# Two small reorderings of a hand-written instruction order: global value products ahead of a routing step, and score steps of the second attention block behind FFN steps

## The chip, the cores and the metric

The kernel runs on one core of a Trainium2 chip. The metric is the device time of one execution in microseconds (us); the time before is the median of three runs. The core has five engines that each work through their own list of instructions in order and wait for one another by semaphores: TensorE (PE in the profile, with its weight loads as PEld), VectorE (DVE), ScalarE (ACT), GpSimd (POOL) and SyncE (SP), which starts most transfers.

## The reference

Three stages follow one another, all in float32:

- **Attention** over 4 batches, 8 heads, 512 local and 32 global tokens per head, head size 64. A local token sees the 32 global keys and the local keys at a distance of at most 32; a global token sees all 544 keys. Softmax, then the product with the values.
- **A dense FFN** on the 2176 resulting tokens of width 512: `h = x @ w_in` (2048 wide), `g = relu(h)**2`, `g @ w_out`.
- **Routed experts**: a token with `x @ w_skip > 0` goes to the one of 8 experts (512 to 1024 to 512, ReLU) with the highest logit `x @ w_gate`, and gets `x + p * y`, where `p` is the softmax probability; the others pass through.

## The kernel before

**Tiles.** Local tokens are cut in 16 tiles of 128, two to a block (`j` = 0 to 7, 256 tokens, `BLK`). Attention runs a tile at a time (`attention(t)`), the FFN a block at a time (`ffn_block(j)`), the routing a tile at a time (`route(t)`); the 32 global tokens of a batch are done in `attention_global(b)`, four heads at a time (`g` = 0, 1). The experts come after all of it, with tokens gathered by index.

**Products in two halves.** Operands of the FFN are split in a high half (`gh`, `xh`, written by a ScalarE cast) and the rest (`gl`, `xl`, a subtraction on GpSimd or VectorE: helper `split`, L203 and L204). A step of the FFN has a first part (`first(f)`: 12 matmuls into `h`, L803 to L805, then a ReLU on ScalarE, L807) and later a second part (`second(f)`: 6 matmuls of 512 columns with `gh` and `gl`, L828 to L830, into `acc`). Between them stand the square (L844 on VectorE or L846 on ScalarE) and the split.

**The order.** Every stage is a generator, and a string of letters says which one moves on by one step: `SEQ` for the start and blocks 0 and 1, `EVEN` for the blocks 2, 4 and 6, `ODD` for 3, 5 and 7. All engines take their order from it, since one step issues instructions on several engines and each engine runs its own in the order in which they were issued. In `SEQ`, `F1`, `E1`, `H1`, `I1` are the next step of the FFN of block 1 (F and I square on VectorE, E and H on ScalarE; F and E subtract on GpSimd, H and I on VectorE), `2a` and `2b` are steps of attention on tiles 4 and 5 (block 2), `R00` and `R01` are routing steps of tiles 0 and 1, `C`, `D` and `A` convert weights, `V` loads values. In `EVEN`, `F` and `E` are FFN steps of the block, `a`, `b`, `g` steps of the attention of the next block, `r` and `s` routing steps of the block before, `V` loads values.

**Steps that matter here.** A call of the FFN in `SEQ` issues by turns the first part of step n, and the square and split of step n with the second part of step n - 1 (in `EVEN` that of step n - 2). Step 1 of `attention` issues the score matmuls (L484), then for the first half: add mask (L497), maximum (L501, L502), four exponentials on ScalarE (L505); the softmax of the second half is step 2. Step 1 of `route` transposes (L300) and casts the high third (L713); step 2 makes the other thirds on VectorE (L703 to L705, and once L719 and on for the weights `w27`); step 3 multiplies (`pl`, L725), then a chain of small VectorE operations (L731 to L747); step 4 has the two prefix matmuls `pr` (L750, L751) and the chain L752 to L776; step 5 the matmul `pt` (L779). Step 3 of `attention_global` has the value products `gpo` and their eviction:

```python
po = ps.tile([P, D], F32, tag=O_TAG, bufs=BANKS[O_TAG], name=f"gpo{b}_{g}")
for c in range(TPB + 1):
    for hh in range(4):
        ...
        nc.tensor.matmul(po[cols, :], ...)
for hh in range(4):
    own = slice(SG * hh, SG * (hh + 1))
    nc.vector.tensor_scalar(
        out=xg[b * SG:(b + 1) * SG, 4 * g + hh], in0=po[own, :], scalar1=rs[own, 2:3], scalar2=None, op0=ALU.mult
    )
```

**Buffers.** `BANKS = {"tr": 2, "s": 1, "o": 1, "h": 2, "x2": 2}` gives the PSUM buffers by tag. In `EVEN`, `gpo`, `pl`, `pr` and `pt` all take the single buffer of tag `o`, in the order in which they are issued: a tile in it can be written only when the one before has been read. `h` of the FFN alternates between two buffers.

Of the kernel before, what the change touches and what calls it, by code (L numbers as in the profile page):

```python
# [22 lines left out]
    0b A V 0a W 0b V A 1q W W A 0b V 1a W W F0 A W E0 1a W W A W V 1a A F0 W 1a I0 A 1b L9 1a H0 V A A W V E0 W 1a  # L23
    X0 H0 A A E0 H0 W H0 A H0 W 1b E0 Lg1 A A W W A E0 1b W H0 A 1b E0 A H0 A E0 Lv00 A W W W 1g A I0 C 1b A 1g I0 W
    A D H0 Lv01 1g W E0 A E0 A I0 1g W C C 1g C W E0 A 1g Lq2 C Lk10 A H0 1g I0 2q A C C F0 2G Lk11 E0 I0 20 C 1b E0 21
    22 F0 F1 23 C D F0 H1 C C V R00 2a F1 D H1 E1 2a E1 D R00 2a H1 R00 R01 C H1 C C F1 I1 R01 V 2b R01 E1 D A F1
    2a E1 D C H1 2b F1 R00 2a I1 C C H1 D F1 V H1 R00 V F1 R01 C Lq3 E1 D E1 C C R01 F1 2b D C 2b H1 C C 1g F1 H1 2b
    2a E1 F1 D E1 F1 H1 Lv10 V 2b I1 V
"""

EVEN = """
    q E F F r E r a F a E lg F s F r E s E F g a s E a E a F g F r V a F g E r V E lv1 F b g s E F b E E b E V g b F
    b F b F g F s lk1 F g E V g lq F lk0 E
"""

# [1673 lines left out]
```

## Time and profile before

| what | value |
|---|---|
| time, median of 3 runs | 692.17 us (690.86 to 692.66) |
| time of the profiled execution | 692.0 us |
| span of the profiled execution, first to last instruction | 690.3 us |
| mean granted TensorE clock | 0.983 |
| busy share PE / PEld / DVE / ACT / POOL | 96 / 80 / 61 / 50 / 26% |

The page gives for each engine its busy time, then the span in 40 slices of 17.3 us (busy tenths, granted TensorE clock in tenths of full speed, transfers). The timeline of the trace lists single instructions of all engines in order of time with their start and duration, and in brackets how long the engine sat idle before one, and for whom it waited. The waits view sums those idle times.

### The profile page before, as it was taken

How to read it: one execution, taken by the hardware profiler on the slowest of the kernel's cores; microseconds unless marked ns; L12 is line 12 of the kernel's file. 1: busy time of each engine (PE TensorE's matmuls, PEld its weight loads, DVE VectorE, ACT ScalarE, POOL GpSimd, SP SyncE). 2: the span in 40 equal slices, each digit the busy share in tenths (PEclk: the TensorE clock that was granted, in tenths of full speed). 3: DMA queues.
4: the chain of work that ended last, by engine and by line, in shares of the span. 5: the costliest groups of instructions: out<-in, count | busy, mean ns of one | idle time of the engine just before them, and what ended most of it. 6: DMA issues, size and time to landing. Idle time of an engine off the chain costs nothing. (4 is left out here: it accounts for less than half of the span.)

```text
span 690.3 us, 16621 instructions
## 1 busy us (share of the span) xinstructions
PE 663.4 (96%) x6545; PEld 553.0 (80%) x6545; DVE 423.2 (61%) x1142; ACT 344.4 (50%) x834; POOL 180.7 (26%) x236
## 2 busy tenths in 40 slices
PE   6689999999999999999999999999999999999996
PEld 4466668788888888888888888888987887898875
DVE  1899983874566377367456647535248535816984
ACT  5767567765534444453445453434344324615862
POOL 8000043354222212312222322222212242301321
PEclk8699999999999999999999999999999999999999
DMA  9999844047053441307243402210056588953920
GB/s 274 248 294 249 282 99 109 1 109 149 5 120 65 95 109 36 85 2 149 72 76 90 108 6 85 82 63 32 1 153 192 200 286 300 385 204 111 371 94 21
DMA packets 137503, 93.39 MB, mean 135 GB/s; under 512 B 103541, under 2 KB 110709, under 8 KB 137412
## 3 DMA queue, kind: packets, MB, share of 16 engines
q1 hardware_dynamic: 127104, 70.62, 38.2%
q10 hardware_dynamic: 8292, 15.48, 6.8%
q0 software_dynamic: 2016, 6.09, 2.5%
q8 instruction: 55, 0.90, 0.6%
q14 instruction: 36, 0.29, 0.1%
HBM read 79.91 MB, written 12.66 MB: 134 GB/s over the span
## 5 line engine op out<-in xcount | busy, mean ns | idle before, releaser
L204 POOL TENSOR_TENSOR gl<-g,gh 128x256 fp32r<-128x256 f32 x107 | 79.8, 746 | 238.7 <-ACT gh L203 94.5
L803 PE MATMUL h<-xh,w_in 128*128 128x256 f32 x464 | 134.1, 289 | 0.0
L805 PE MATMUL h<-xh,w_in 128*128 128x256 f32 x464 | 129.8, 280 | 0.2 <-POOL w_in L275 0.2
L804 PE MATMUL h<-xl,w_in 128*128 128x256 f32 x464 | 129.6, 279 | 0.0
L828 PE MATMUL acc<-w_out,gh 128*128 128x512 f32 x232 | 97.0, 418 | 1.2 <-ACT gh L203 1.2
L830 PE MATMUL acc<-w_out,gl 128*128 128x512 f32 x232 | 91.9, 396 | 0.2
L829 PE MATMUL acc<-w_out,gh 128*128 128x512 f32 x232 | 91.5, 395 | 0.0
L803 PEld LDWEIGHTS h<-xh,w_in 128*128 128x128 f32 x464 | 87.1, 188 | 4.5 <-issue 1.0
L804 PEld LDWEIGHTS h<-xl,w_in 128*128 128x128 f32 x464 | 87.2, 188 | 2.7 <-DVE xl L204 0.2
L805 PEld LDWEIGHTS h<-xh,w_in 128*128 128x128 f32 x464 | 87.1, 188 | 0.4 <-POOL w_in L275 0.4
L807 ACT ACTIVATE g<-h 128x256 f32<-128x256 f32 x128 | 48.7, 380 | 66.8 <-PE h L805 45.1
L203 ACT CAST gh<-g 128x256 fp32r<-128x256 f32 x116 | 47.1, 406 | 37.7 <-DVE g L844 35.6
L844 DVE TENSOR_TENSOR g<-h,g 128x256 f32<-128x256 f32 x53 | 22.1, 417 | 69.5 <-ACT g L807 69.4
L505 ACT ACTIVATE sm<-sm,mx 128x128 f32<-128x128 f32 x120 | 41.2, 391 | 43.1 <-DVE mx L502 43.1
L830 PEld LDWEIGHTS acc<-w_out,gl 128*128 128x128 f32 x232 | 43.5, 188 | 12.0 <-POOL gl L204 1.5
L828 PEld LDWEIGHTS acc<-w_out,gh 128*128 128x128 f32 x232 | 43.6, 188 | 8.4 <-ACT gh L203 1.7
L829 PEld LDWEIGHTS acc<-w_out,gh 128*128 128x128 f32 x232 | 43.7, 189 | 5.8
L275 POOL TENSOR_TENSOR w_in<-st_raw_in,w_in 128x512 fp32r<-128x512 f32 x10 | 13.2, 1326 | 74.7 <-ACT w_in L271 74.7
L497 DVE TENSOR_TENSOR sm<-sc,masks_slots 128x512 f32<-128x512 f32 x30 | 20.6, 687 | 14.7 <-PE sc L484 13.5
L846 ACT ACTIVATE g<-g 128x256 f32<-128x256 f32 x63 | 26.2, 415 | 4.1 <-ACT g L807 2.1
L826 PE MATMUL acc<-st_raw_out,gh 128*128 128x512 f32 x48 | 23.9, 618 | 0.8 <-ACT gh L846 0.8
L511 PE MATMUL ptr<-ident,sm 128*128 128x128 f32 x120 | 20.5, 290 | 2.5 <-ACT sm L505 2.4
(649 smaller groups left out, 1446.3 us busy)
## 6 DMA issues: line engine op xcount, KB each, us to landing
st_e<-in_moe_w_dram SPq DMA_DIRECT2D x46, 512.0 KB
st_raw_in<-in_moe_w_in_dram SPq DMA_DIRECT2D x16, 512.0 KB
st_raw_out<-in_moe_w_out_dram SPq DMA_DIRECT2D x16, 512.0 KB
st_e<-in_moe_w_dram ACTq DMA_DIRECT2D x12, 512.0 KB
x2d<-x ACTq DMA_DIRECT2D x19, 256.5 KB
vr<-in_v_l_dram SPq DMA_DIRECT2D x32, 128.0 KB
st_gv<-in_v_l_dram SPq DMA_DIRECT2D x8, 512.0 KB
out_dram<-x ACTq DMA_DIRECT2D x16, 256.0 KB
```

What stands on the lines that cost most here:

```text
L203: nc.scalar.copy(hi, src)
L204: (lo_engine or nc.vector).tensor_tensor(out=lo, in0=src, in1=hi.bitcast(F32), op=ALU.subtract)
L505: nc.scalar.activation(sm[:, hh, :], sm[:, hh, :], AF.Exp, bias=mx[:, hh:hh + 1], scale=SCALE, **sums)
L803: nc.tensor.matmul(h, lhsT=wh, rhs=xh[:, k, :], start=(k == 0), stop=False)
L804: nc.tensor.matmul(h, lhsT=wh, rhs=xl[:, k, :], start=False, stop=False)
L805: nc.tensor.matmul(h, lhsT=wl, rhs=xh[:, k, :], start=False, stop=(k == KD - 1))
L807: nc.scalar.activation(g, h, AF.Relu)
L826: nc.tensor.matmul(acc[z], lhsT=gh[:, c], rhs=w, start=first_one, stop=last_one)
L828: nc.tensor.matmul(acc[z], lhsT=gh[:, c], rhs=wh, start=first_one, stop=False)
L829: nc.tensor.matmul(acc[z], lhsT=gh[:, c], rhs=wl, start=False, stop=False)
L830: nc.tensor.matmul(acc[z], lhsT=gl[:, c], rhs=wh, start=False, stop=last_one)
L846: nc.scalar.activation(square, g, AF.Square)
```

## The change

Only the order strings change; nothing is computed differently, and no transfer changes its place on SP's or any other queue.

```diff
-    22 F0 F1 23 C D F0 H1 C C V R00 2a F1 D H1 E1 2a E1 D R00 2a H1 R00 R01 C H1 C C F1 I1 R01 V 2b R01 E1 D A F1
-    2a E1 D C H1 2b F1 R00 2a I1 C C H1 D F1 V H1 R00 V F1 R01 C Lq3 E1 D E1 C C R01 F1 2b D C 2b H1 C C 1g F1 H1 2b
+    22 F0 F1 23 C D F0 H1 C C V R00 F1 2a D H1 E1 2a E1 D R00 2a H1 R00 R01 C H1 C C F1 I1 R01 V R01 E1 2b D A F1
+    2a E1 D C H1 F1 2b R00 2a I1 C C H1 D F1 V H1 R00 V F1 R01 C Lq3 E1 D E1 C C R01 F1 2b D C 2b H1 C C 1g F1 H1 2b
...
-    q E F F r E r a F a E lg F s F r E s E F g a s E a E a F g F r V a F g E r V E lv1 F b g s E F b E E b E V g b F
+    q E F F r E r a F a E lg F s F r E s E F g a s E a E a F g F g r V a F E r V E lv1 F b g s E F b E E b E V g b F
```

**In `EVEN` (three blocks) on TensorE.** `gpo` are the global value products, `pr` the prefix matmuls of the routing, `h_8` and `acc` the FFN. The piece of the difference for block 2, around the end of the first part of FFN step 8:

```order
 L805 MATMUL h_8_2784<-xh_2260,w_in_2_2131 128x256
+L626 MATMUL gpo_0_2799<-st_gv_0_2328,gpT_0_2778 32x64 x16
+L626 MATMUL gpo_0_2799<-vgr_2330,gpTg_0_2782 32x64 x4
 L750 LDWEIGHTS tri
-L750 MATMUL pr_2799<-oh_2573,tri 128x8
+L750 MATMUL pr_2824<-oh_2573,tri 128x8
 L751 LDWEIGHTS ones
-L751 MATMUL pr_2799<-oh_2573,ones 128x8
+L751 MATMUL pr_2824<-oh_2573,ones 128x8
 L828 MATMUL acc_2427<-w_out_1988,gh_6_2680 128x512
```

The value products stood behind the six `acc` matmuls that follow `pr`; now they stand directly ahead of `pr`, and the six matmuls behind it. On VectorE the four evictions of `gpo` (L634) move from behind the routing chain and the FFN's square to ahead of the chain, between the copy of `gpTg` (L619) and L752.

**In `SEQ` on ScalarE, first place.** `sm` are the exponentials of tile 4, `x2T` the routing's cast, `gh_13` and `gh_14` the high halves of the FFN's steps 13 and 14 of block 1, `w_out` a weight conversion:

```order
 L713 CAST x2T_1525<-x2tr_1520 128x512
-L505 ACTIVATE sm_0_1562,osum_1527<-sm_0_1562,mx_0_1564 128x128 x4
-L203 CAST gh_13_1571<-g_13_1506 128x256
+L203 CAST gh_13_1527<-g_13_1506 128x256
+L505 ACTIVATE sm_0_1575,osum_1540<-sm_0_1575,mx_0_1577 128x128 x4
 L271 CAST w_out_1584<-st_raw_out_371 128x512
 L807 ACTIVATE g_14_1600<-h_14_1587 128x256
 L846 ACTIVATE g_14_1600<-g_14_1600 128x256
 L203 CAST gh_14_1602<-g_14_1600 128x256
```

The four exponentials and the cast of `gh_13` change places. On TensorE the six `acc` matmuls of step 12, which stood behind the score matmuls of tile 4, now stand ahead of them, directly behind the transposes `x2tr`; on VectorE the square of step 13 goes ahead of the mask and maximum of tile 4.

**In `SEQ`, second place, on ScalarE.** `rt` is the softmax of the routing of tile 1 and `sm_0` the exponentials of tile 5:

```order
 L807 ACTIVATE g_1_1747<-h_1_1734 128x256
-L505 ACTIVATE sm_0_1792,osum_1757<-sm_0_1792,mx_0_1794 128x128 x4
-L743 ACTIVATE rt_1814<-rt_1814 128x8
+L743 ACTIVATE rt_1770<-rt_1770 128x8
 L846 ACTIVATE g_1_1747<-g_1_1747 128x256
-L203 CAST gh_1_1827<-g_1_1747 128x256
+L203 CAST gh_1_1783<-g_1_1747 128x256
+L505 ACTIVATE sm_0_1829,osum_1794<-sm_0_1829,mx_0_1831 128x128 x4
```

The four exponentials of tile 5 go behind the high half of FFN step 1 (`gh_1`). On TensorE the score matmuls of tile 5 stood between `h_1` and the routing matmuls `pl` of tile 1; now `h_1`, `pl`, the six `acc` matmuls of step 0 and then the scores follow one another. A few steps on, the softmax of tile 5's second half and the square and cast of step 3 change places in the same way.

## Rows read from the trace of the kernel before

**Rows 1.** The page: busy time of the engines, and the granted clock by slice.

```profile
PE 663.4 (96%) x6545; PEld 553.0 (80%) x6545; DVE 423.2 (61%) x1142; ACT 344.4 (50%) x834; POOL 180.7 (26%) x236
...
PEclk8699999999999999999999999999999999999999
```

**Rows 2.** Waits of TensorE, 60 to 700 us: total, times, longest.

```profile
PE gpo L626 <- DVE sizes L766: 1.0, 3, 0.4
```

**Rows 3.** Timeline of block 2's piece: start, duration, instruction, idle time before it.

```profile
198.04 0.67 DVE L615 COPY gpT<-gptr 128x512 f32<-128x512 f32 x1
...
198.46 0.18 PE L750 MATMUL pr<-oh,tri 128*128 128x8 bf16 x1
...
200.52 0.49 PEld L626 LDWEIGHTS gpo<-st_gv,gpT 128*32 128x32 f32 x32 [0.79 <-DVE sizes L766]
...
203.12 0.19 PEld L779 LDWEIGHTS pt<-ohs,ohl 128*128 128x128 f32 x1 [0.29 <-DVE xg L634]
```

**Rows 4.** Timeline of the first place of `SEQ`, all engines.

```profile
116.06 1.16 PE L484 MATMUL sc<-kT,qT 64*32 64x128 f32 x64
116.25 0.41 ACT L203 CAST gh<-g 128x256 fp32r<-128x256 f32 x1
...
116.69 0.43 DVE L204 TENSOR_TENSOR gl<-g,gh 128x256 fp32r<-128x256 f32 x1 [1.60 <-ACT gh L203]
...
117.14 0.50 PE L828 MATMUL acc<-w_out,gh 128*128 128x512 f32 x1
...
118.95 0.40 ACT L505 ACTIVATE sm<-sm,mx 128x128 f32<-128x128 f32 x1 [0.41 <-DVE mx L502]
...
120.51 0.39 ACT L203 CAST gh<-g 128x256 fp32r<-128x256 f32 x1
120.80 0.65 ACT L271 CAST w_out<-st_raw_out 128x512 fp32r<-128x512 f32 x1
120.95 0.50 PE L828 MATMUL acc<-w_out,gh 128*128 128x512 f32 x1 [0.74 <-ACT gh L203]
...
122.22 0.41 ACT L203 CAST gh<-g 128x256 fp32r<-128x256 f32 x1
...
122.81 0.28 PE L803 MATMUL h<-xh,w_in 128*128 128x256 f32 x1
...
124.58 0.48 PE L828 MATMUL acc<-w_out,gh 128*128 128x512 f32 x1
...
124.98 0.20 DVE L705 TENSOR_TENSOR w<-w,w 128x36 bf16<-128x36 f32 x1
...
125.55 1.31 POOL L275 TENSOR_TENSOR w_out<-st_raw_out,w_out 128x512 fp32r<-128x512 f32 x1 [2.12 <-ACT w_out L271]
...
125.76 0.41 ACT L203 CAST gh<-g 128x256 fp32r<-128x256 f32 x1
...
126.06 0.46 PE L725 MATMUL pl<-w,x2T 128*128 128x27 bf16 x12
126.20 0.94 DVE L204 TENSOR_TENSOR gl<-g,gh 128x256 fp32r<-128x256 f32 x1 [0.43 <-ACT gh L203]
```

**Rows 5.** Timeline of block 6's second `gpo`, which no routing step follows.

```profile
455.90 0.65 PE L626 MATMUL gpo<-st_gv,gpT 128*32 128x64 f32 x32
...
456.73 0.50 PE L828 MATMUL acc<-w_out,gh 128*128 128x512 f32 x1
456.85 1.18 DVE L634 TENSOR_SCALAR xg<-gpo,grs 32x64 f32<-32x64 f32 x4 [2.00 <-PE gpo L626]
```

**Rows 6.** Timeline of the second place of `SEQ`.

```profile
131.18 1.16 PE L484 MATMUL sc<-kT,qT 64*32 64x128 f32 x64
...
131.91 0.69 DVE L705 TENSOR_TENSOR x2T<-x2tr,x2T 128x512 bf16<-128x512 f32 x1
...
136.89 0.50 PE L828 MATMUL acc<-w_out,gh 128*128 128x512 f32 x1 [0.48 <-ACT gh L203]
...
138.57 0.40 PE L830 MATMUL acc<-w_out,gl 128*128 128x512 f32 x1
```

## The prediction

> **What bounds the kernel now.** I read the page first: TensorE is busy for 663.4 us of the 690.3 us span, 96%, no other engine is above 61% apart from TensorE's own weight loads, and the granted clock is low only in the first two of the 40 slices [rows 1]. So after the start the span is the sum of what TensorE has to do and of the short times for which it stands still, and a change of order can win or lose only in those. Next I read the waits of TensorE from 60 us on: they are few and small, and one kind belongs to this change, the global products `gpo`, which wait three times, 1.0 us together, for the VectorE chain of the routing (L766) [rows 2]. Last I read the timeline at the three kinds of place that the diff touches, to see who ends last there; the sums below are made from it. The stages after the blocks are untouched, and as TensorE bounds them too, what is lost or won here passes to the end.
>
> **EVEN: what is removed.** `gpo` and `pr` share the one buffer `o`. Before, `pr` ran at 198.46 without a wait, the six FFN products behind it, and then `gpo` waited until the routing chain had read `pr`: TensorE's idle time is 1.0 / 3 = 0.33 us [rows 2] and that of its weight loads 0.79 [rows 3]. Matmul ends are modelled, so the true loss lies between these; I take 0.5. Later `pt` waited for the eviction of `gpo`, 0.29 by the weight loads [rows 3]; I take 0.27, since `pt` now has only `pr` ahead of it in the buffer. Removed: 0.8 a block, bounds 0.6 and 1.1.
>
> **EVEN: what is added.** `gpo` comes right behind the first part of step 8, where `pr` stood at 198.46. It needs `gpT`, whose copy ends at 198.04 + 0.67 = 198.71 [rows 3]: with about 0.05 for the semaphore (`gh` ends at 120.51 + 0.39 = 120.90 and its matmul starts at 120.95 [rows 4]) a wait of 0.30. Then `pr` must wait until `gpo` is evicted, and only four small VectorE operations can do that. A `gpo` without a route behind it shows how long this takes: it starts at 455.90, TensorE is through with it at 456.73 (0.83), VectorE starts the evictions at 456.85 (0.95 after the start) and needs 1.18 [rows 5]. So the buffer is free 0.95 + 1.18 + 0.05 = 2.18 after `gpo` starts, and TensorE stands still for 2.18 - 0.83 = 1.35. The six FFN products that covered this gap before now stand behind `pr`, and TensorE goes in order. Everything queued there waits: the products, the next first part, `pt`. On VectorE the routing chain, the square of step 8 and its cast come about 2 us later; step 8's halves are used only two products on, and the chain has those products and a first part, about 3 us, to finish before `pt`, so I cost that at nothing (bound: 0.3 a block, if the chain ends late). Added: 0.30 + 1.35 = 1.65. Net +0.85 a block, bounds +0.5 and +1.2; three blocks **+2.55** (1.5 to 3.6).
>
> **SEQ, first place.** Removed is the wait of the products of step 13 for `gh_13`, which stood behind four exponentials on ScalarE: 0.74 by TensorE's idle time, and its low half comes late too, so that the six products take 120.95 to 122.81, 1.86, against 124.58 to 126.06, 1.48, for those of step 14 [rows 4]. Added, in the order in which it comes:
>
> - The products of step 12 would start at 116.06, but `gh_12` ends at 116.25 + 0.41 = 116.66: they start at 116.71, 0.65 late, and end 1.5 later at 118.2. The scores follow, 2.15 later than before.
> - The first exponential came 118.95 - 116.06 = 2.89 after the scores' start, so it now comes at 121.1. `gh_13` is out before it, so step 13 runs without a wait. But everything behind the exponentials on ScalarE is late by 2.15 less the 0.29 of the cast that went ahead (120.51 to 120.80): 1.86. `gh_14` started at 122.22 and now starts at 124.08 and ends at 124.49.
> - Step 14's products start at 124.54. TensorE would have been there at about 124.0 (118.2 + 1.08 for the scores, 1.5 for `h_14`, 1.48, and 122.81 to 124.58 for `h_15` with four transposes), so the wait that was at step 13 is now at step 14. With the low half late in the same way they take 1.86 and end at 126.4, not 126.06.
> - `pl` of tile 0 needs the routing weights (L705, ended at 124.98 + 0.20 = 125.18), behind a VectorE list which waits for the ScalarE cast (120.80) that is 1.86 late: 126.9 to 127.0. `pl` starts there, **0.9 later** than 126.06.
>
> **SEQ, second place.** `h_1` ended where the scores began, at 131.18; with the 0.9 it ends at 132.1. Now `pl` of tile 1 comes next, and its last third (L705) was ready at 131.91 + 0.69 = 132.60 even in the old order, behind the scores that covered it. It hangs on a chain through `gh_15`, the routing of tile 0, the cast of `x2T` and back to VectorE: 132.60 - 125.76 = 6.84 from the start of `gh_15` [rows 4, 6]. `gh_15` came 3.54 behind `gh_14`, of which about 0.3 was waiting for TensorE: it now starts at 127.3 to 127.6, and the third is ready at 134.1 to 134.5, or 133.6 if the `gl` in the chain takes 0.43 as at 116.69 and not 0.94 as at 126.20 [rows 4]. So TensorE stands still for 1.5 to 2.4, and I take 2.0. Then come the last ten `pl` matmuls (0.3), the products of step 0 (1.48), the scores (1.08), `h_2` with the transposes (1.77), the products of step 1 (1.48) with no wait for `gh_1`: from 134.1, 6.1 together, 140.2. Before, they ended at 138.57 + 0.23 = 138.8, after the wait of 0.48 [rows 6]. The first place's 0.9 has become **+1.3** (0.8 to 2.0). The swap a few steps on leaves TensorE's order as it is, and VectorE and ScalarE are ahead there by more than the lag: nothing (bound 0.4).
>
> [...] The `gl` that lasted 0.94 at 126.20 ran while GpSimd converted a weight from 125.55 to 126.86, the one at 116.69 with no GpSimd work beside it [rows 4]. [...]
>
> **The sum.** 692.0 is the profiled execution's time (span 690.3 and 1.7 around it), 0.2 below the median. 692.0 + 2.55 + 1.3 = **695.9**, 0.55% slower. A measurement of this kernel can tell about 0.3%, 2.1 us, from no change.
>
> **Rivals.**
> - *SEQ pays, EVEN does not.* Its place is `pl` of tile 1: if its last third is ready by 132.1, when `h_1` ends, TensorE does not stop there, and with step 14 and `pl` of tile 0 unhindered too `SEQ` gives back the waits it had, up to 0.74 + 0.38 at step 13 and about as much at step 1, less 0.65 at step 12: some -0.7 to -1.6. The time is 692.0 + 2.55 - 1.0 = 693.5, no measurable change. It decides from the point where the chain is 2 us faster than in the old trace; for it speaks only that ScalarE and VectorE are idle between; against it, that each link's order is fixed.
> - *Faster.* If `pr` did not have to wait for the evictions (1.35 away, so each block -0.5) and `SEQ` gave -1.0: 692.0 - 1.5 - 1.0 = 689.5. The order of the buffer `o` speaks against it.
> - *More than that.* The lag of VectorE meets GpSimd's conversions again at later steps of `SEQ` and EVEN's chain ends after `pt` is due: +2.0 for `SEQ`, +3.6 for EVEN: 697.6.
> [...]
>
> **How the numbers follow.** Forecast 0.64 (694.2 to 697.5); SEQ pays 0.17 (692.6 to 694.2); faster 0.05; more 0.10 (697.5 to 699); clock 0.04. The range 693.0 to 698.5 leaves out the faster case, the clock and the ends of the others, about 2 in 10. Slower by over 0.3% (above 694.3): 0.64 + 0.10 + 0.04 = 0.78, less a little for the edge, 0.76; within 0.3% 0.19; faster 0.05.
>
> **What would show it.** In the changed profile: `pr` waiting for `xg` L634 three times, near 1.35 us each, and no wait of `gpo` for L766 or of `pt` for L634; `gpo` waiting about 0.3 for `gpT`; no wait of step 13's products for `gh`, but one at step 14; the first exponential of tile 4 near 121.1; `pl` of tile 0 near 126.9 and a wait of 1.5 to 2.4 at `pl` of tile 1 for L705; block 2 starting about 1.3 late, and each even block adding 0.85. I would be wrong if the evictions of `gpo` started earlier than its last matmul, if ScalarE reached the exponentials without holding up `gh_14`, or if TensorE's idle times at these places were not on the path to the end.

## The result and the profile after

The changed kernel takes 699.76 us (median of 6 runs, 698.21 to 701.26) against 692.17 before: ratio 1.0113, interval 1.0094 to 1.0131. It is slower, as forecast, but by 7.6 us and not by 3.7, and the time lies above the range. Its profiled execution took 699.13 us, 7.1 more than that of before (692.0).

The page, with the rows that answer to [rows 1]:

```profile
PE 666.5 (96%) x6545; PEld 555.4 (80%) x6545; DVE 420.2 (60%) x1142; ACT 344.3 (49%) x834; POOL 178.2 (26%) x236
...
PEclk9799999999999999999999999999999999999999
```

TensorE is busy 3.1 us longer with the same 6545 matmuls, and the span is 7.1 longer: most of the loss is standing still, but not all. The waits of TensorE from 60 to 700 us (total, times, longest), for [rows 2]:

```profile
PE pr L750 <- DVE xg L634: 3.8, 3, 1.3
PE acc L828 <- ACT gh L203: 1.8, 4, 0.7
PE pl L725 <- DVE x2T L704: 1.2, 1, 1.2
...
PE pl L725 <- DVE x2T L705: 0.5, 1, 0.5
PE pl L725 <- DVE w L705: 0.4, 1, 0.4
```

The wait of `gpo` for L766 is gone; `pr` waits three times for the evictions, `pl` waits in `SEQ`, and `acc` waits for `gh` four times instead of twice. These sums don't say where the time is lost for good. For that, set the start of a matmul in this trace against the start of the same one before. At the transposes of tile 0 (115.47 us before) this execution is 0.01 late; at `pr` of tile 0 (141.62), 2.47; at `pt` of tile 0 (148.53), 3.43; at the second `pr` of block 2 (207.33), 5.69; at that of block 4 (322.43), 6.38; at that of block 6 (437.55), 7.05; and at the last `pr` before the experts (547.91), 7.06. So everything is lost in five stretches (the first holds two places), and nothing is given back behind them. Each can be followed in the timeline (start, duration, instruction, idle time before it).

The first place of `SEQ`, for [rows 4]:

```profile
116.72 0.50 PE L828 MATMUL acc<-w_out,gh 128*128 128x512 f32 x1 [0.58 <-ACT gh L203]
...
121.16 0.40 ACT L505 ACTIVATE sm<-sm,mx 128x128 f32<-128x128 f32 x1 [2.31 <-DVE mx L502]
...
124.12 0.41 ACT L203 CAST gh<-g 128x256 fp32r<-128x256 f32 x1
...
124.58 0.50 PE L828 MATMUL acc<-w_out,gh 128*128 128x512 f32 x1 [0.25 <-ACT gh L203]
...
126.73 0.20 DVE L705 TENSOR_TENSOR w<-w,w 128x36 bf16<-128x36 f32 x1
126.98 0.45 PE L725 MATMUL pl<-w,x2T 128*128 128x27 bf16 x12 [0.39 <-DVE w L705]
```

The second place, for [rows 6]:

```profile
131.99 0.19 PE L725 MATMUL pl<-w,x2T 128*128 128x27 bf16 x1
...
133.40 0.19 PE L725 MATMUL pl<-w,x2T 128*128 128x27 bf16 x1 [1.22 <-DVE x2T L704]
...
134.12 0.41 PE L725 MATMUL pl<-w,x2T 128*128 128x27 bf16 x10 [0.54 <-DVE x2T L705]
...
138.81 0.40 ACT L505 ACTIVATE sm<-sm,mx 128x128 f32<-128x128 f32 x1 [1.76 <-DVE mx L502]
...
141.77 0.40 ACT L203 CAST gh<-g 128x256 fp32r<-128x256 f32 x1
...
142.22 0.50 PE L828 MATMUL acc<-w_out,gh 128*128 128x512 f32 x1 [0.24 <-ACT gh L203]
...
143.05 0.50 PE L830 MATMUL acc<-w_out,gl 128*128 128x512 f32 x1
...
144.09 0.18 PE L750 MATMUL pr<-oh,tri 128*128 128x8 bf16 x1
```

Behind the four exponentials (138.81) now stands `gh_2` (141.77), and the products of step 2 wait for it (142.22) and for the `gl` behind it (143.05). A few steps on, the third swap:

```profile
143.59 0.42 DVE L844 TENSOR_TENSOR g<-h,g 128x256 f32<-128x256 f32 x1 [1.86 <-ACT g L807]
143.93 0.68 DVE L497 TENSOR_TENSOR sm<-sc,masks_slots 128x512 f32<-128x512 f32 x1
...
145.23 1.31 POOL L275 TENSOR_TENSOR w_out<-st_raw_out,w_out 128x512 fp32r<-128x512 f32 x1
...
145.36 1.20 DVE L502 TENSOR_SCALAR mx<-mx 128x4 f32<-128x4 f32 x1
...
146.60 0.40 ACT L505 ACTIVATE sm<-sm,mx 128x128 f32<-128x128 f32 x1 [2.15 <-DVE mx L502]
...
148.16 0.36 ACT L807 ACTIVATE g<-h 128x256 f32<-128x256 f32 x1
...
149.99 0.40 ACT L203 CAST gh<-g 128x256 fp32r<-128x256 f32 x1
...
150.44 0.50 PE L828 MATMUL acc<-w_out,gh 128*128 128x512 f32 x1 [0.69 <-ACT gh L203]
```

The same stretch before the change:

```profile
138.18 0.68 DVE L497 TENSOR_TENSOR sm<-sc,masks_slots 128x512 f32<-128x512 f32 x1
...
139.61 1.07 DVE L502 TENSOR_SCALAR mx<-mx 128x4 f32<-128x4 f32 x1
...
140.76 0.39 ACT L505 ACTIVATE sm<-sm,mx 128x128 f32<-128x128 f32 x1
...
144.51 0.38 ACT L807 ACTIVATE g<-h 128x256 f32<-128x256 f32 x1 [1.82 <-PE h L805]
```

The mask of the second half (L497) has to wait for the square of `h_3` and comes 5.75 later than before. The small step behind its maximum (L502) takes 1.20 us for 128 x 4 elements, beside a conversion on GpSimd, where it took 0.17 at 120.95 with none beside it; but that is not new, since at this place it took 1.07 before. So the exponentials come 5.84 later than before, directly in front of the ReLU of `h_4`, for which ScalarE had stood waiting before (1.82), and the products of step 4 wait for their high half.

Block 2, for [rows 3]:

```profile
202.27 0.65 PE L626 MATMUL gpo<-st_gv,gpT 128*32 128x64 f32 x32 [0.15 <-DVE gpT L615]
...
203.22 1.16 DVE L634 TENSOR_SCALAR xg<-gpo,grs 32x64 f32<-32x64 f32 x4 [0.82 <-PE gpo L626]
...
204.43 0.17 PE L750 MATMUL pr<-oh,tri 128*128 128x8 bf16 x1 [1.27 <-DVE xg L634]
...
204.48 0.48 PE L828 MATMUL acc<-w_out,gh 128*128 128x512 f32 x1
...
205.08 0.63 PE L830 MATMUL acc<-w_out,gl 128*128 128x512 f32 x1
...
208.45 0.28 PE L805 MATMUL h<-xh,w_in 128*128 128x256 f32 x1
```

And the busy time there by stretches of 2 us (PE, PEld, DVE, ACT, POOL, then the granted clock, the transfers' share and GB/s):

```profile
202.00:204.00 2.00, 1.01 (x41) 0.74 (x41) 1.15 (x5) 0.38 (x1) 1.59 (x2) 1.00 0.79 223
204.00:206.00 2.00, 1.57 (x7) 1.25 (x7) 1.75 (x15) 0.00 (x0) 0.00 (x0) 0.74 1.33 234
206.00:208.00 2.00, 2.00 (x9) 1.81 (x8) 0.91 (x4) 0.41 (x1) 0.58 (x1) 0.50 0.51 87
208.00:210.00 2.00, 2.00 (x14) 1.81 (x13) 0.30 (x1) 0.39 (x1) 0.15 (x1) 0.91 0.14 23
```

After a stop of 1.27 us the granted clock was still 1.00 when the first two products started (0.48 and 0.49 us); from 204.96 to 208.37 it was 0.50: a product takes 0.63, and that is a part of the added busy time. Behind the same stop in blocks 4 and 6 (`pr` at 321.76 and 437.55) it stayed at 1.00, and the third product took 0.39 or 0.40.

### The profile page after: what moved, and what is told of

Same layout as the page of the kernel before. It is cut to its first block, busy times and chain, and to the rows that moved or that the text cites. A ratio compares the mean times of both kernels' runs of the same rounds, so it can differ in the third digit from the quotient of the medians.

```text
span 697.4 us, 16627 instructions
## 1 busy us (share of the span) xinstructions
PE 666.5 (96%) x6545; PEld 555.4 (80%) x6545; DVE 420.2 (60%) x1142; ACT 344.3 (49%) x834; POOL 178.2 (26%) x236
## 5 line engine op out<-in xcount | busy, mean ns | idle before, releaser
L497 DVE TENSOR_TENSOR sm<-sc,masks_slots 128x512 f32<-128x512 f32 x30 | 20.6, 686 | 17.7 <-PE sc L484 16.9
```

## The experiments

The table puts the loss of each trace where it arises: the start of a matmul less its start in the trace before, and of that the growth over each stretch, in us. The five stretches end at `pr` of tile 0 (141.62), `pt` of tile 0 (148.53), and the second `pr` of blocks 2, 4 and 6; the first begins at 115.47. Traces repeat to about 0.05 there. A fall of the granted clock from 1.00 to 0.50 is marked *. In e6 and e7 `gpo` is in another buffer. e8 lost another 3.7 ahead of 115.47.

| kernel | first two places | third swap | block 2 | block 4 | block 6 | ratio (interval) |
|---|---|---|---|---|---|---|
| changed | 2.46 | 0.96 | 2.26* | 0.69 | 0.67 | 1.0113 (1.0094 to 1.0131) |
| e1 EVEN alone | 0.0 | 0.0 | 0.65 | 0.66 | 0.68 | 1.0038 (1.0024 to 1.0052) |
| e2 SEQ alone | 2.43 | 0.93 | 0.0 | 0.0 | 0.0 | 1.0062 (1.0049 to 1.0076) |
| e3 first move | 1.43 | 0.0 | 0.0 | 0.0 | 0.0 | 1.0025 (1.0016 to 1.0034) |
| e4 second move | 1.02 | 0.11 | 0.0 | 0.0 | 0.0 | 1.0015 (1.0006 to 1.0024) |
| e5 third move | 0.0 | 0.72 | 0.04 | 0.0 | 0.0 | 1.0012 (1.0003 to 1.0021) |
| e6 EVEN, other buffer | 0.0 | 0.0 | 0.02 | 0.03 | 0.02 | 0.9996 (0.9987 to 1.0005) |
| e7 before, other buffer | 0.0 | 0.0 | -0.80 | -0.77 | -0.76 | 0.9965 (0.9952 to 0.9978) |
| e8 evictions twice | 0.0 | 0.0 | 3.51* | 3.51* | 1.99 | 1.0219 (1.0203 to 1.0235) |
| e9 as e1 | 0.0 | 0.0 | 2.18* | 0.71 | 0.66 | one run |
| e10 as e1 | 0.0 | 0.0 | 2.19* | 0.69 | 0.68 | one run |
| e11 as changed | 4.00* | 0.94 | 2.21* | 0.67 | 0.67 | one run |
| e12 as changed | 2.45 | 0.93 | 2.20* | 0.69 | 0.67 | one run |
| e13 EVEN in 4 and 6 | 0.0 | 0.0 | 0.0 | 0.70 | 0.66 | 1.0025 (1.0015 to 1.0036) |
| e14 EVEN in 6 | 0.0 | 0.0 | 0.0 | 0.03 | 0.68 | 1.0011 (1.0001 to 1.0021) |
| e15, e16 as e13, e14 | 0.0 | 0.0 | 0.0 | 0.69; 0.02 | 0.66; 0.67 | one run each |

**The halves.** The `EVEN` half alone, and the `SEQ` half alone (the three moves, each shown below, with the old `EVEN`):

```diff
-    a E a F g F r V a F g E r V
+    a E a F g F g r V a F E r V
```

> Only the EVEN half of the change (the global value products ahead of the routing step in blocks 2, 4 and 6), the start sequence as before. Theory A (each block loses the wait of pr for the evictions, 1.27, and 0.15 at gpo, less some 0.75 of waits removed): +0.67 in each of three blocks, 2.0 together, about 694.2; the clock fell in block 2 of the changed kernel by chance of where the wait lay, and where it falls again that block costs 1.5 more. Theory B (the wait of pr behind block 2's start takes the clock down every time): +0.67 x 3 + 1.5 = 3.5 or, if in all three blocks, 6.5: 695.7 to 698.7. Theory C (the EVEN half is nearly free and the whole loss is the start's): under 692.8.

> Only the three moves in the start sequence, EVEN as before. Theory A (the moves add what the matmuls of the routing and of the second parts show in the trace of the changed kernel at the end of the sequence, 3.45): about 695.6, TensorE's work of block 2 about 3.45 late at its first routing step, then no further loss, and no clock fall in blocks 2, 4 and 6 since pr does not wait there. Theory B (the start's loss was partly caused by the clock): under 694.5.

Measured: 695.17 us and 696.66 us. They add up (1.0038 x 1.0062 = 1.0100, inside the interval of the change). In the traces `EVEN` costs 0.66 a block as long as the clock holds, and `SEQ` 3.4: theory A for both. The medians are about 1 us above theory A's 694.2 and 695.6; for `EVEN` the falls of the clock in e9 and e10 below are a likely reason, for `SEQ` e11 has a possible reason, but no second trace of `SEQ` alone was taken.

**The first two moves of `SEQ`, one at a time.**

```diff
-    22 F0 F1 23 C D F0 H1 C C V R00 2a F1 D H1 E1 2a
+    22 F0 F1 23 C D F0 H1 C C V R00 F1 2a D H1 E1 2a
```

> Only the first move (second products of step 12 and square and split of step 13 ahead of the scores of tile 4). Theory A (the loss stands at this place and is passed on unchanged): pl of tile 0 about 0.9 late, and 0.9 at the end of the start sequence: 693.1. Theory B (the lag of ScalarE and VectorE grows at the next scores): 1.5 to 2.5 late at the end: 693.7 to 694.7. Theory C (the later waits absorb it): under 0.3 late, 692.4.

```diff
-    F1 I1 R01 V 2b R01 E1 D A F1
+    F1 I1 R01 V R01 E1 2b D A F1
```

> Only the second move (routing matmuls pl of tile 1 and the second products of step 0 ahead of the scores of tile 5). Theory A (two parts: pl stands for about 1.2 for its last third, ready at 132.6, which the waits it removes at step 1 just pay back; then the exponentials hold up the high half of step 2 and its products wait, 0.86 as in the changed kernel): 0.7 to 1.0 late at the end of the start sequence, 693.0. Theory B (the second move costs the whole 1.57 that it cost in the changed kernel, whether or not the first move is there): 693.7.

Measured: 693.81 and 693.26 us. The first move alone is 1.43 late at `pr` of tile 0, between theories A and B: `pl` of tile 0 starts at 127.01, 0.9 late with its offset taken off, and at the second place half a microsecond more is lost, since the last third of tile 1 is late too (`pl` waits 0.54 there and not 0.18). The second move alone loses 1.02 there and 1.13 in all, nearest to theory A. The timeline of e4 shows both of its parts:

```profile
132.00 0.19 PE L725 MATMUL pl<-w,x2T 128*128 128x27 bf16 x1 [0.66 <-DVE x2T L704]
132.72 0.41 PE L725 MATMUL pl<-w,x2T 128*128 128x27 bf16 x10 [0.54 <-DVE x2T L705]
...
137.41 0.40 ACT L505 ACTIVATE sm<-sm,mx 128x128 f32<-128x128 f32 x1 [1.77 <-DVE mx L502]
...
140.83 0.50 PE L828 MATMUL acc<-w_out,gh 128*128 128x512 f32 x1 [0.24 <-ACT gh L203]
```

**The third move.**

```diff
-    2a E1 D C H1 2b F1 R00 2a I1
+    2a E1 D C H1 F1 2b R00 2a I1
```

> Only the third move (softmax of the second half of tile 5 behind square and split of step 3). Theory A (the mask and maximum of that half now wait for the square of h_3 and meet GpSimd's conversion, so the exponentials come in front of the ReLU of h_4, and the products of step 4 wait for their high half): about 0.96 late at pt of tile 0, as in the changed kernel: 693.1. Theory B (this came only of the delays that the first two moves had made): under 0.3 late, under 692.5.

Measured: 692.74 us; 0.72 is lost at `pt`, most of theory A's 0.96. L502 takes 1.19 here, at 142.41 (1.07 before the change), the exponentials start at 143.63, and the products of step 4 wait 0.46. So it is a loss of the swap itself; the first two moves only made it larger. The three single moves sum to 1.46 + 1.13 + 0.77 = 3.36, as much as they cost together (3.4).

**Taking `gpo` out of the shared buffer.** In both kernels below `gpo` gets the buffer of the scores (`s`) instead of `o`, for the first with the order of the change in `EVEN`, for the second with that of before:

```diff
-    def attention_block(j, S_TAG="s", O_TAG="o", G_TAGS=("s", "o")):
+    def attention_block(j, S_TAG="s", O_TAG="o", G_TAGS=("s", "s")):
```

> EVEN as in the change, the start sequence as before, and the global value products in the buffer of the scores (tag s) instead of the one that pr and pt use, so pr need not wait until they are evicted. Theory A (that wait is the whole price of the EVEN half): no wait at pr, no clock fall in blocks 2, 4 and 6, each block 0.76 less the 0.15 of gpo for gpT, 0.6 faster than before: 690.3. Theory B (the evictions ahead of the routing chain on VectorE cost as much, since the chain now ends too late for pt): pt waits about 1 each time, and the time is 692 or more.

> The order of before in both strings, and the global value products in the buffer of the scores. Theory A (in the old order the shared buffer costs both the wait of gpo for the routing chain, 0.5, and that of pt for the evictions, 0.27): both waits gone, 0.75 a block, 2.2 together: 690.0. Theory B (pt waits for its operands rather than for the buffer, so only gpo's wait goes): 0.45 a block, 690.8.

Measured: e6 691.62 us, no change from before; e7 689.45 us, 2.4 faster by the ratio. In e6 `pr` doesn't wait, so that stop comes of the shared buffer, as forecast. But the shared buffer is not the whole price of the move: e7 has the buffers of e6 in the old order, and against it the move still costs 0.8 a block (0.02 against -0.78), more than the 0.66 with the shared buffer. The evictions now hold up the routing chain on VectorE, and `pt` waits for its last operation, three times (theory B's mechanism, at 0.4 by the matmuls and 0.6 by the weight loads, and not 1). The timeline of e6:

```profile
199.06 0.18 PE L750 MATMUL pr<-oh,tri 128*128 128x8 bf16 x1
...
202.18 0.34 DVE L776 TENSOR_SCALAR ohl<-iota_s,rt 128x128 fp32r<-128x128 f32 x1
...
202.57 0.33 PE L779 MATMUL pt<-ohs,ohl 128*128 128x136 f32 x1 [0.39 <-DVE ohl L776]
```

In e7 the waits view has no wait of TensorE's matmuls in blocks 2 to 6, and each block is 0.76 to 0.80 shorter: theory A. It beats both kernels.

**A longer stop.** The evictions are done twice, with the same values:

```diff
-            for hh in range(4):
+            for hh in (0, 1, 2, 3, 0, 1, 2, 3):
                 own = slice(SG * hh, SG * (hh + 1))
```

> EVEN as in the change alone, with each eviction of the global value products done twice (the same values written again), so that pr waits 1.18 longer, about 2.45. Theory A (pr's wait is on the path in full and a longer stop of TensorE takes the clock down more often): each even block 0.66 + 1.18 = 1.84 late, 5.5 together, and the clock falls in most of the three blocks behind it, 1.5 each: 699 to 702. Theory B (the clock fall in block 2 of the changed kernel has nothing to do with the length of that stop): the waits alone, 697.7, and low clock in no more than one block.

Measured: 706.78 us. The three waits of `pr` are 7.8 together, 2.6 each. The clock fell behind those of blocks 2 and 4, not behind that of block 6; theory A in kind, and 1.5 for each fall. The time is above its range because the start doubles its evictions too, which I had not counted: 3.7 is lost ahead of 115 us, nearly all between 91 and 97, with a stop of 2.6 ahead of 95.42 (`gptr` for `pg`) and low clock (0.50) from 96.7 to 100.1. The stretches behind the three `pr` (columns as above):

```profile
206.00:208.00 2.00, 2.00 (x6) 1.52 (x5) 1.75 (x11) 0.08 (x1) 0.00 (x0) 0.50 0.42 80
...
326.00:328.00 2.00, 2.00 (x11) 2.00 (x11) 0.51 (x2) 0.40 (x1) 0.74 (x1) 0.50 0.56 100
...
442.00:444.00 2.00, 1.32 (x8) 1.10 (x8) 1.75 (x13) 0.00 (x0) 0.00 (x0) 1.00 1.02 378
```

**More traces of the same kernels.** To see whether the fall goes with `pr`:

> The EVEN half alone once more, for one more trace. Its five runs before lie in two groups, 693.4 and 693.5 against 695.2 to 695.5, and the trace at hand is of the first group, with three waits of 1.27 at pr and full clock behind each. Theory A (one fall of the clock behind one of the waits of pr makes the difference of some 1.7): a run near 695.3 shows one low stretch of 3 to 5 us directly behind a pr of block 2, 4 or 6, one near 693.5 shows none. Theory B (the groups come of the start or of the experts): a run near 695.3 has full clock in the blocks and its routing steps of block 7 some 1.6 behind the kernel before, as in the trace at hand.

> As the run before it, the same kernel again: theory A asks for the same link of time and low stretch, theory B for none.

> The changed kernel once more. Theory A (each of the three waits of pr can be followed by a fall of the clock, not always the same): the time is 692.0 + 3.45 + 2.0 = 697.5 plus about 1.5 for each low stretch behind a pr, and the low stretches lie behind pr and nowhere else after the first 45 us, not always in block 2. Theory B (the fall belongs to block 2): low clock behind the pr of block 2 again, and in no other block.

> As the run before it, the same kernel again: the time goes by the number of low stretches (theory A), or block 2 and no other has one (theory B).

Measured: 695.29, 694.21, 701.15 and 698.89 us. All four fell behind the `pr` of block 2, and none behind that of block 4 or 6, so this fall is one reason why the kernel's own times spread (theory A of e9). It is not the only one: e10 has it too, at a time between the groups; at the last `pr` it is as late as e9 (2.81 and 2.74), and the two part behind it, among the experts. "Not always the same" is not borne out. The stretch behind the `pr` of block 2 in e9, with the fall, and in e1, without:

```profile
202.00:204.00 2.00, 2.00 (x10) 1.90 (x9) 0.58 (x2) 0.40 (x1) 0.73 (x1) 0.50 0.52 88
...
202.00:204.00 2.00, 2.00 (x17) 1.91 (x16) 1.23 (x6) 0.61 (x2) 0.42 (x1) 1.00 0.68 113
```

e11 fell once more, behind the 1.25 and 0.54 for which `pl` of tile 1 stands, and lost 1.5 there:

```profile
132.00:134.00 2.00, 0.22 (x3) 0.10 (x2) 1.87 (x3) 1.12 (x3) 2.00 (x3) 1.00 0.00 0
134.00:136.00 2.00, 2.00 (x15) 1.66 (x16) 1.37 (x10) 0.23 (x2) 0.52 (x1) 0.63 0.00 0
136.00:138.00 2.00, 2.00 (x51) 1.35 (x53) 0.00 (x0) 0.88 (x4) 0.72 (x1) 0.51 0.00 0
```

**The first stop, or block 2?** The move in blocks 4 and 6 only, and in block 6 only (`EVEN` of before for the other even blocks; with `j < 6` in the place of `j == 2` for the second):

```diff
-            for what in (ODD if j % 2 else EVEN).split():
+            for what in (ODD if j % 2 else EVEN if j == 2 else EVEN.replace("g F r V a F g E", "g F g r V a F E")).split():
```

> The EVEN half of the change in blocks 4 and 6 only; block 2 and the start as before. Theory A (the fall of the clock follows the first stop of 1.27 after a long stretch without one): block 4 shows low clock behind its pr, so 2 x 0.66 + 1.5 = 2.8 late at the end, 694.9. Theory B (it belongs to block 2's place in the program): full clock in all blocks, 1.3 late, 693.4.

> The EVEN half of the change in block 6 only. Theory A (first stop): low clock behind the pr of block 6, 0.66 + 1.5 = 2.2 late, 694.2. Theory B (block 2's place): full clock in all blocks, 0.7 late, 692.8.

> The move in blocks 4 and 6 once more, for a second trace. Theory A: low clock behind the pr of block 4 again. Theory B: none.

> The move in block 6 once more, for a second trace. Theory A: low clock behind the pr of block 6. Theory B: none.

Measured: 694.12, 693.28, 693.94 and 694.28 us. No trace has low clock behind a `pr` (it was granted 1.00 there); the losses are the 0.66 to 0.70 a block of the waits alone. That is what theory B forecast, but it doesn't show the reason that it gives (see Open). (e16 is as late as its one block makes it, 0.68, up to the experts; its other 2 us arose behind them, at places that the change doesn't touch.)

## Why the prediction was wrong

**Right: what bounds it, and the direction.** Each stop of TensorE at the three places of the diff came through to the end in full: 3.50 late at 188.62, behind `SEQ`, and from block 6 on 7.05 without change. The first place went as worked out, link by link: products of step 12 at 116.72 (116.71 forecast), first exponential at 121.16 (121.1), `gh_14` at 124.12 (124.08), its products at 124.58 (124.54), `pl` of tile 0 at 126.98 (126.9 to 127.0).

**Right, a little too high: `EVEN`.** Removed 0.8 a block: e7, which takes just those waits away, gains 0.76 to 0.80. Added 1.65: VectorE starts the evictions 0.95 after `gpo`, `pr` comes 2.16 after it (2.18 forecast) and waits 1.27 (1.35), and `gpo` waits 0.15 for `gpT` (0.30); 1.42 together. The net is 0.66 and not 0.85, 2.0 for three blocks and not 2.55. That the later routing chain costs nothing held only because `pr` and all behind it are late as well: in e6, without that stop, it costs 0.4 at `pt`, over the bound of 0.3.

**Wrong: "the first place's 0.9 has become +1.3".** The last third of tile 1 came as forecast (`pl` at 134.12; 134.1 forecast), and the last product of step 1 started at 140.18, 1.61 after its 138.57 in [rows 6] and 0.2 later than the sum had it (which gives 1.4 by its own numbers, 140.2 less 138.8, where I wrote 1.3). But there the sum stopped, one step too early. At the first place I had followed the four exponentials to the next high half behind them and found the wait moved from step 13 to step 14; at the second I wrote "with no wait for `gh_1`" and did not look at `gh_2`, which stands behind those exponentials in the same way. TensorE waits for it and for its low half, and at `pr` the lag is 2.47: 0.9 more. In e4 the same wait of 0.24 stands at 140.83, without the first move.

**Wrong: "the swap a few steps on leaves TensorE's order as it is ...: nothing (bound 0.4)".** It costs 0.96, alone 0.72. I judged it by TensorE's order and by how far ahead the other engines were before. The swap itself used that lead up: mask and maximum stand behind a square that had not come yet, so the exponentials come 5.84 later, 3.37 more than the lag of 2.47. ScalarE's lead ahead of the ReLU of `h_4` was 1.82; now the ReLU waits for the exponentials and starts at 148.16, 1.18 later than the lag alone would have it. GpSimd is no new cause here: L502 stood beside a conversion before the change as well (1.07, now 1.20); what the swap would cost without it no run shows. L502 ends at 146.56 and GpSimd's conversion at 146.54, and it took 0.17 at 120.95 with no GpSimd work beside it; what holds it up there was not shown. The `gl` that took 0.94 before the change, at 126.20, took 0.94 again, at 127.67, beside a conversion from 127.02.

**Wrong in size and place: the clock, 0.04.** I allowed for it only at the longest stop, `pl` of tile 1, with a loss of 7 us, which no run shows; each fall that was measured cost 1.5. It came behind the `pr` of block 2, in five of six traces with that stop (the changed kernel, e1, e9 to e12; not in e1), and once in four at `pl` (the changed kernel, e2, e11, e12). The falls of the table all lie behind a stop (1.27 or 2.6 at `pr`, 1.25 and 0.54 at `pl` in e11); but behind 19 of 24 stops of 1.27 at `pr` there was none, and the forecast gave no reason to expect one in block 2.

The sum with what was measured: 692.0 + 3.4 (`SEQ`) + 2.0 (`EVEN`) + 1.5 (clock) = 698.9, against 699.13 for the profiled execution. It missed by 3.2: 2.1 too little for the two steps of `SEQ`, 1.5 for the clock, and 0.55 too much for `EVEN`, 3.05 together. The rival *More than that* (697.6) lies nearer, but not for its reasons: it had `EVEN` at +3.6, which cost 2.0, and put `SEQ` at +2.0 for GpSimd's conversions, beside which VectorE took long before as well (1.07 at L502, 0.94 for `gl`). The median is 0.6 higher than that execution; a second fall as in e11 could account for some of the runs, but they have no traces.

**Open.** Why the clock falls behind the stop in block 2 and not behind the same stop of 1.27 in blocks 4 and 6 (none in 18) is not settled. The four traces e13 to e16 speak against its being the first such stop, and e8, where block 4 fell as well behind 2.6, against its being block 2 alone. Nor can the block be all of it, since e1, without a fall, is the same kernel as e9 and e10. One rival was left untested, and the traces speak for it. The times at which the granted clock changes lie on one even scale of 3.41 us within a trace (17.22, 20.64, 24.05, 27.46, 34.29, 204.96 and 208.37 us in the changed kernel; 4.71, 8.12, 14.95, 21.77 and 32.02 in e1), and this scale lies differently against the program in each. Carried on along the trace, `pr` of block 2 starts 0.82 to 0.91 of the way from one mark of the scale to the next in the five traces that fell, and 0.39 in e1; in blocks 4 and 6 it starts at 0.11 to 0.52 in all 18 cases. So the fall may go with where the stop lies on that scale and not with the block; e13 to e16 don't tell the two apart. More traces of one kernel would.

## What to carry to other kernels

When a group of instructions is put behind another on an in-order engine, follow it to the next one that now stands behind it, at every place where it is moved and not only at the first: here the wait moved on by a step at both (0.74 at step 13 became 0.25 at step 14, 0.48 at step 1 became 0.24 at step 2) and did not go away. A product that shares a single buffer with the next one should not be put directly ahead of it; the work that stood between hid the evictions (without it `pr` waited 1.27). Another buffer took that stop away but not the price of the move, since the evictions then stood ahead of a chain that the next product waited for (0.39 by the matmuls at `pt` in e6); the other buffer in the old order (e7) gained more than any order tried here. A swap that leaves the order of the bounding engine alone still had a price, since it made a helper wait for an input that came later (0.72 in e5).

## What the runs showed of the hardware

- A stop of TensorE of 1.27 us was followed by 3.4 us (204.96 to 208.37 in the changed kernel) at a granted clock of 0.50 instead of 1.00, at a cost of 1.5 us, in block 2 in five of six traces and in blocks 4 and 6 in none of 18 cases; stops of 2.6 were followed by it in three of four places (e8). What decides is open.
- TensorE's idle time in the trace before understated what two waits cost: at `gpo` of the even blocks the matmuls show 1.0 us in all, the weight loads 2.3 there and 0.9 at `pt`; taking both waits away gained 2.3 (e7).
- A VectorE operation on 128 x 4 elements (L502) took 1.20 us instead of 0.17 beside a conversion on GpSimd (the changed kernel; 1.19 in e5, 1.07 in the kernel before).
